# Reordering the first stage of a fused attention, expert and feed-forward kernel: tables and loads, products, scatters, and a PSUM bank for VectorE

## The chip, the cores and the metric

The kernel runs on one core of a Trainium2 chip. The metric is the time of one execution on the device in microseconds (us). In the rows PE is TensorE, PEld its weight loads, DVE VectorE, ACT ScalarE, POOL GpSimd, SP SyncE (which here issues most DMAs; SPq is its queue).

## The reference

Three computations follow one another, all in fp32. A recurrence over time with a state per head, then a mixture of 8 experts of which each token goes to one, then a gated feed-forward block.

```python
for t in range(S):                      # B=2, H=8, S=768, D=48
    cur = einsum('bhd,bhe->bhde', u * k[t], v[t])
    y[t] = einsum('bhd,bhde->bhe', r[t], state + cur)
    state = w * state + einsum('bhd,bhe->bhde', k[t], v[t])
x = y.transpose(0, 2, 1, 3).reshape(1536, 384)
logits = x @ w_gate; e = argmax(logits); gate = softmax(logits)[e]
x = gate * (relu(x @ w1[e]) @ w2[e])    # 8 experts, F=1024; up to `capacity` tokens each
g = x @ w_gate2
out = (g * sigmoid(g) * (x @ w_val)) @ w_out
```

## The kernel before

**Attention and routing (up to about 87 us).** The 1536 tokens are cut into NT = 12 tiles of 128, six (NCH) per batch. One loop, `for it in range(-4, NT + 1)` (L366 to L429), is a software pipeline: in iteration `it` it works on several tiles at once. For tile it+4 POOL makes the products `diag_pool` (L239 ruk = r*k, L240 ruk = ruk*u, L242 kd = k times powers of w), and SP loads r and k (`load_rk`, L131) into one of three buffers that these products have read before. For tile it+3 DVE scales the transposed r and k (`decay`, L234, RK) and sums ruk into the diagonal c (`diag_dve`, L246), and ACT writes 16 diagonal blocks (`diag_act`, L255). For tile it+2 TensorE forms A (`inner`, L262), of which DVE copies the lower triangle (L269), and the state's increment U (L277). The state Z is updated by DVE (L288) and POOL (L289). For tile `it` TensorE forms y (`outputs`, L297 and L303), ACT copies it to xT (`d_major`, L310), and TensorE turns it to token order with the logits beside it (`token_major`, L470, xl, in PSUM under the tag "xt" with two buffers). For tile it-1 `logits` sums the logits on DVE (L477, lg) and copies xu on ACT (L479).

Routing comes in groups of tiles, BATCHES = (0,3), (3,6), (6,8) and then one tile at a time. `route1` (L481 to L497) finds the expert by some small DVE operations (m, dif L491, eqr, oh L497) on lg, `place_pe` counts with TensorE (L510), `route2` (L514 to L543) gives each token its row in a table x_disp in DRAM. Each tile's x is then scaled by its gate on ACT (L550) and written to its rows by an indirect DMA that POOL issues (`scatter`, L551). `send()` does one such scatter at the start of an iteration, ahead of that iteration's work on POOL. The table has 1760 rows per expert, of which BLK = 224 are read at first.

The scatters are a chain: all write x_disp, and each waits for the one before to land. After scatter 7 the rows of expert 0 are loaded into xr0 (`x_load`, L625, on SP); scatter 8 waits for that load, and scatters 9, 10 and 11 follow. The load of expert 1's rows, xrs[1], here called xr1, waits for scatter 11. The rows of the last four tiles are added to expert 0's input by TensorE itself (`first_add`, L341), with xr0's rows (`first_rows`, L349).

**Experts (from about 87 us).** For each of 8 experts f runs over 8 steps up (`up_plain` L772 for expert 0, then L760) with a relu (L779 on ACT, L780 on DVE), and 8 steps down (L749, L750). The weights come in units, "raw" buffers of 128x768, RAWS = 10 of them, loaded on SP (`unit_load`, L606). `prefetch` (L642) loads units 0 to 7, one per iteration from it = 3 on; two more are loaded at the start of the experts. DVE and ACT split each unit into a high and a low part (L616, L617). At f = 0 of expert 0 `order()` (L805 and L898) does some small DVE work on the counts, at f = 1 `places()` (L815) and the load of xr1, at f = NF+3 = 11 `x_turn` transposes xr1 (L741).

**Feed-forward (to the end).** Products with w_gate, w_val and w_out, fed by what the experts left in DRAM.

The order of each engine's instructions is the order in which the code calls them; no scheduler changes it. The functions that the change touches:

Of the kernel before, what the change touches and what calls it, by code (L numbers as in the profile page):

```python
# [22 lines left out]
P = 128  # L23
# [24 lines left out]
RAWS, WS = 10, 6  # L48

# [15 lines left out]
class Kernel:  # L65
# [46 lines left out]
    def attention(self, st):  # L112
# [57 lines left out]
        Wm = tp.tile([P, HP, D], F32, name="Wm")  # L170
# [19 lines left out]
        nc.vector.tensor_copy(mask, tmpm)  # L190
        W2 = tp.tile([P, 2, HP, P], F32, name="W2")
# [13 lines left out]
        pbad = ps_1.tile([P, 1], F32, name="pbad", tag="xt", bufs=2)  # L205
# [14 lines left out]
        wps = ps_1.tile([P, HP, 2, 64], F32, name="wps", tag="xt", bufs=2)  # L220
# [6 lines left out]
        self.xl, self.xu, self.batches, self.to_scatter = {}, {}, BATCHES, []  # L227
# [8 lines left out]
        def diag_pool(i):  # L236
            r_t, k_t = rk[i % NB][:, 0], rk[i % NB][:, 1]
            ruk = ruks[i] = tp.tile([P, DM], F32, name="ruk", tag="ruk", bufs=2)
            nc.gpsimd.tensor_mul(ruk, r_t, k_t)  # L239
            nc.gpsimd.tensor_mul(ruk, ruk, u_b)  # L240
            if i % NCH < NCH - 1:
                nc.gpsimd.tensor_mul(kds[i % NB], k_t, wk_tok)  # L242

        def diag_dve(i):
            c = cc[i] = tp.tile([P, 2, HP], F32, name="c", tag="c", bufs=3)
            nc.vector.tensor_reduce(  # L246
                c.rearrange("p j h -> p h j"), ruks.pop(i).rearrange("p (h j d) -> p h j d", j=2, d=D), AX.X, ALU.add
            )
# [33 lines left out]
        def state_update(i):  # L282
            zn, hd = Z[(i + 1) % 2], slice(0, 64 + D)
            if i % NCH == 0:
                nc.vector.tensor_mul(zn[hd], U[hd], Wm[hd])
            else:
                zt = tp.tile([P, HP, D], F32, name="zt", tag="zt", bufs=2)
                nc.vector.tensor_add(zt[hd], U[hd], Z[i % 2][hd])  # L288
                nc.gpsimd.tensor_mul(zn[hd], zt[hd], Wm[hd])  # L289
# [24 lines left out]
        self.route_rooms()  # L314
        self.ones_bf = cp.tile([P, P], BF16, name="ones_bf")
# [11 lines left out]

        def late_tables():
            nc.vector.tensor_copy(Wm, sq[:, 7].unsqueeze(2).to_broadcast([P, HP, D]))
            self.route_tables(wg, tmpm, rev_i, cap_i)  # L330
            nc.vector.memset(self.ones_bf, 1.0)
# [26 lines left out]
        def send():  # L358

            if self.to_scatter:  # L360
                i = self.to_scatter[0][0]
                self.scatter()
                if i == NT - NLAST - 1:
                    self.x_load(0, self.xr0)

        for it in range(-4, NT + 1):  # L366

            send()
            batch = ends.get(it - 1)
            late = it - 1 >= NT - LATE  # L370
            if ok(it):
# [3 lines left out]
            if ok(it - 1):  # L375
                self.logits(it - 1)
# [17 lines left out]
            if it < 0 and ok(it + 3):  # L394
                decay(it + 3)
                load_T(it + 3 + NB)
            if ok(it + 3):
                diag_dve(it + 3)
                diag_act(it + 3)
            if ok(it + 4):  # L400
                diag_pool(it + 4)
                load_rk(it + 4 + NB)
            if ok(it + 2):
# [3 lines left out]
            if it >= 0 and ok(it + 3):  # L407
                decay(it + 3)
                load_T(it + 3 + NB)

            if it == NT - 5 or it == NT - 3:
                send()
# [13 lines left out]
            if it >= 3:  # L426
                self.prefetch(it - 3)
# [12 lines left out]

    def route_rooms(self):
# [3 lines left out]
        self.rev = tp.tile([P, E], F32, name="rev")  # L445
# [4 lines left out]
    def route_tables(self, wg, tmpm, rev_i, cap_i):  # L450
# [6 lines left out]
        nc.vector.tensor_copy(self.IW[:, :, 2 * D:], wg.rearrange("p (h e) -> p h e", e=E))  # L457
        nc.vector.tensor_copy(self.before, tmpm)
        nc.vector.tensor_copy(self.rev, rev_i)
        nc.vector.tensor_scalar(  # L460
            out=self.cap_f, in0=cap_i[:, 0:1], scalar1=float(E * ST), scalar2=None, op0=ALU.add
        )
        nc.vector.memset(self.ex[:, :, E:], 1e-9)
# [8 lines left out]
    def logits(self, i):  # L472
        nc, tp, xl = self.nc, self.tp, self.xl.pop(i)
        t = i - max(lo for lo, _ in self.batches if lo <= i)
        if t == 0:
            self.lg = tp.tile([P, NBT, E], F32, name="lg", tag="lg", bufs=2)
# [4 lines left out]
    def route1(self, lo, hi):  # L481
# [14 lines left out]
        nc.vector.tensor_reduce(m[:, 1], eqr, AX.X, ALU.max)  # L496
        nc.vector.tensor_tensor(oh, eqr, b3(m[:, 1]), ALU.is_equal)  # L497
# [16 lines left out]
    def route2(self, lo, hi):  # L514
# [3 lines left out]
        nc.vector.reciprocal(m[:, 2], m[:, 2])  # L518
# [7 lines left out]
            out=m[:, 3], in0=place, scalar=self.cap_f, in1=m[:, 2], op0=ALU.is_lt, op1=ALU.mult  # L526
        )

        def rows(out):
            nc.vector.scalar_tensor_tensor(  # L530
                out=out, in0=m[:, 1], scalar=-float(ST), in1=place, op0=ALU.mult, op1=ALU.add
# [13 lines left out]
    def scatter(self):  # L545
# [4 lines left out]
        self.nc.scalar.activation(xs, xu, AF.Copy, scale=scale)  # L550
        self.nc.gpsimd.indirect_dma_start(  # L551
            out=self.x_disp, out_offset=bass.IndirectOffsetOnAxis(ap=self.row[:, i:i + 1], axis=0), in_=xs,
            in_offset=None,
        )

# [86 lines left out]
    def prefetch(self, k):  # L642

        if k < 8:
            self.unit_load(0, k)
# [186 lines left out]
    def experts(self, st):  # L832
# [34 lines left out]
        n_loaded, n_split = 8, 1  # L867
# [171 lines left out]
    def general(self):  # L1039
# [3 lines left out]
        with ExitStack() as ss:  # L1043
# [13 lines left out]
            nc.gpsimd.iota(rev_i, pattern=[[-1, E]], base=E, channel_multiplier=0)  # L1057
            self.route_rooms()
# [122 lines left out]
```

## Time and profile before

| | us |
|---|---|
| median of 3 runs | 468.25 |
| lowest, highest | 466.6, 471.62 |
| the profiled execution | 467.29 |
| its span | 465.6 |
| mean granted clock of TensorE | 0.977 of full speed |

The rows of the trace come from the one profiled execution; its span is the time from its first to its last instruction, and the sums are made against its own 467.29 us. TensorE is busy for 437.9 us of the span (94%), VectorE for 295.4, ScalarE for 213.0, POOL for 173.8. [...]

### The profile page before, as it was taken

Reading aid. Unit: us, or ns where it says so; the run is one execution under the profiler, and the core shown is the slowest. Engines: PE = TensorE matmul, PEld = TensorE weight load, DVE = VectorE, ACT = ScalarE, POOL = GpSimd, SP = SyncE. Lnnn points to the kernel's source line nnn. Section 1 sums busy time; section 2 is a strip of 40 time slices with the busy share of each in tenths; the row PEclk is TensorE's granted clock in tenths of the full one; section 3 lists DMA queues with packets and bytes.
Section 4 is the critical chain, followed back from the end, with each engine's and each line's share of the span. In section 5 each row is a group of like instructions: output and inputs, shape, how many; then the busy total and the mean of one; then the engine's idle time right before and its main releaser. Section 6 shows DMA issues by size and latency. Waiting matters only on the chain. (4 is left out here: it accounts for less than half of the span.)

```text
span 465.6 us, 8417 instructions
## 1 busy us (share of the span) xinstructions
PE 437.9 (94%) x3211; PEld 422.6 (91%) x3211; DVE 295.4 (63%) x566; ACT 213.0 (46%) x469; POOL 173.8 (37%) x159
## 2 busy tenths in 40 slices
PE   7899959986999999999999999999999999999991
PEld 7688847876999999999998999999999999999991
DVE  6869778585798798889466698989857111111110
ACT  1667755452675666666455554334244032130310
POOL 6987563140111120000044445665454433233321
PEclk9799989998999999999999999999999999999998
DMA  7787931539998998750101333324300000100001
GB/s 261 254 285 249 337 132 59 186 117 288 360 328 206 283 295 203 265 195 1 69 1 68 137 86 119 126 78 136 124 14 1 34 18 1 52 0 35 19 18 39
DMA packets 24802, 63.78 MB, mean 137 GB/s; under 512 B 4784, under 2 KB 10032, under 8 KB 24752
## 3 DMA queue, kind: packets, MB, share of 16 engines
q1 hardware_dynamic: 22112, 57.43, 38.0%
q0 software_dynamic: 1920, 4.73, 2.8%
q10 hardware_dynamic: 720, 1.00, 0.9%
q8 instruction: 27, 0.44, 0.4%
q14 instruction: 23, 0.19, 0.1%
HBM read 55.67 MB, written 7.48 MB: 136 GB/s over the span
## 5 line engine op out<-in xcount | busy, mean ns | idle before, releaser
L984 POOL TENSOR_TENSOR al<-sg,ah 128x384 fp32r<-128x384 f32 x48 | 54.2, 1129 | 138.7 <-ACT ah L983 138.7
L617 DVE TENSOR_TENSOR wlo<-raw,whi 128x768 fp32r<-128x768 f32 x60 | 57.2, 954 | 12.2 <-ACT whi L616 10.1
L749 PE MATMUL py<-hc,whi 128*128 128x448 f32 x192 | 64.6, 377 | 0.0
L983 ACT CAST ah<-sg 128x384 fp32r<-128x384 f32 x48 | 24.7, 514 | 78.1 <-DVE sg L980 78.1
L760 PE MATMUL A<-xc,whi 128*128 128x224 f32 x336 | 56.6, 274 | 0.0
L750 PE MATMUL py<-hc,wlo 128*128 128x256 f32 x192 | 54.6, 284 | 0.0
L760 PEld LDWEIGHTS A<-xc,whi 128*128 128x128 f32 x336 | 51.1, 192 | 0.1
L616 ACT CAST whi<-raw 128x768 fp32r<-128x768 f32 x60 | 49.9, 838 | 2.8 <-DMA raw<-in_w 2.1
L997 PE MATMUL po<-w_out_hi,ah 128*128 128x384 f32 x144 | 48.6, 337 | 0.0
L999 PE MATMUL po<-w_out_hi,al 128*128 128x384 f32 x144 | 48.5, 337 | 0.0
L998 PE MATMUL po<-w_out_lo,ah 128*128 128x384 f32 x144 | 48.5, 337 | 0.0
L760 PE MATMUL A<-xc,wlo 128*128 128x224 f32 x168 | 46.2, 275 | 0.0
L749 PEld LDWEIGHTS py<-hc,whi 128*128 128x128 f32 x192 | 36.9, 192 | 2.7
L1006 DVE TENSOR_TENSOR acc<-acc,po 128x384 f32<-128x384 f32 x36 | 19.3, 546 | 30.9 <-PE po L999 30.9
L827 POOL DMA_INDIRECT ids<-tok,by_expert x12 | 14.6, 1213 | 62.7 <-DMA ids<-tok,by_expert 57.6
L980 DVE TENSOR_TENSOR sg<-A,sg 128x384 f32<-128x384 f32 x24 | 13.3, 554 | 37.9 <-PE A L977 30.2
L750 PEld LDWEIGHTS py<-hc,wlo 128*128 128x128 f32 x192 | 37.3, 194 | 0.0
L980 DVE TENSOR_TENSOR sg<-g,sg 128x384 f32<-128x384 f32 x24 | 13.3, 555 | 34.5 <-PE g L977 29.7
L255 ACT ACTIVATE AT<-ident,c 128x128 f32<-128x128 f32 x96 | 29.4, 390 | 11.7 <-DVE c L246 11.7
L779 ACT ACTIVATE hc<-A 128x224 fp32r<-128x224 f32 x64 | 23.1, 362 | 23.3 <-PE A L760 19.0
L760 PEld LDWEIGHTS A<-xc,wlo 128*128 128x128 f32 x168 | 32.3, 192 | 0.0
L979 ACT ACTIVATE sg<-A 128x384 f32<-128x384 f32 x24 | 11.7, 486 | 34.7 <-PE A L977 34.7
(171 smaller groups left out, 1132.1 us busy)
## 6 DMA issues: line engine op xcount, KB each, us to landing
raw<-in_w SPq DMA_DIRECT2D x62, 384.0 KB, 6.7
rkT<-in_rkT SPq DMA_DIRECT2D x12, 512.0 KB, 5.4
rk<-in_rk SPq DMA_DIRECT2D x12, 384.0 KB, 3.8
raw<-in_w_gate SPq DMA_DIRECT2D x6, 768.0 KB, 4.3
raw<-in_w_val SPq DMA_DIRECT2D x6, 768.0 KB, 4.5
raw<-in_w_out SPq DMA_DIRECT2D x6, 768.0 KB, 4.4
x_disp<-zero SPq DMA_DIRECT2D x8, 336.0 KB, 6.2
xr<-x_disp SPq DMA_DIRECT2D x8, 336.0 KB, 5.7
```

Source lines behind the costliest of these rows:

```text
L255: nc.scalar.activation(AT[i][:, j, hp], ident, AF.Copy, scale=c[:, j, hp:hp + 1])
L616: nc.scalar.copy(h_, raw)
L617: nc.vector.tensor_sub(l_, raw, h_.bitcast(F32))
L749: nc.tensor.matmul(ps[:, 0:2 * BLK], lhsT=wh, rhs=xc, start=first, stop=False, skip_group_check=True)
L750: nc.tensor.matmul(ps[:, 0:256], lhsT=wl, rhs=xc[:, 0:256], start=False, stop=last, skip_group_check=True)
L760: self.nc.tensor.matmul(ph[:, HI], lhsT=w[:, k, fs], rhs=x[1][:, k, half], start=(k == 0 and i == 0), stop=(k == KD - 1 and i == 2),)
L980: nc.vector.tensor_mul(sg, pg["w_val"], sg)
L983: nc.scalar.copy(h_, sg)
L984: nc.gpsimd.tensor_sub(l_, sg, h_.bitcast(F32))
L997: nc.tensor.matmul(po, lhsT=ah[:, ts_], rhs=wh, start=(i == 0), stop=False)
L998: nc.tensor.matmul(po, lhsT=ah[:, ts_], rhs=wl, start=False, stop=False)
L999: nc.tensor.matmul(po, lhsT=al[:, ts_], rhs=wh, start=False, stop=(i == len(parts) - 1))
```

## The change

The names in the changed kernel's rows are of its own lines. The parts:

- **Tables.** The tables for routing, which `late_tables` made in iteration -3 (L329 to L331, L453 to L463), are made before the powers of w; what needs w_gate and the capacity (`route_inputs`) comes in iteration -1. The tile Wm, w spread over the state, is gone: the multiplies read it by a broadcast from sq.
- **A bank in PSUM** (`psum_rooms`) holds lg, rev, the rank and the sum of routing, and u (`u_ps`). The buffers of the tag "xt" go from two to one.
- **Products.** ruk = ruk*u goes from POOL to DVE (in `diag_dve`); POOL's order is now ruk, the state's decay, kd.
- **Scatters.** `scale` (ACT) stays at the start of an iteration, `issue` (the DMA) comes at its end, behind the products, and only for the last iterations at once.
- **x ahead of the outputs.** `logits` (with xu's copy) comes before `outputs`; tile 2's diagonal comes behind xT in iteration 0; `inner` comes earlier in the iterations below 0.
- **Loads.** All ten raw units are loaded in iterations 3 to 8, ahead of xr0.
- **order() and places()** go from f = 0 and 1 to f = 3 and 5.

```diff
+PREFETCH = {3: [0], 4: [1], 5: [2], 6: [3], 7: [4, 5], 8: [6, 7, 8, 9]}
...
+        u_ps = self.psum_rooms(True)
+        self.route_rooms()
+        self.route_tables(tmpm, rev_i)
+        self.ones_bf = cp.tile([P, P], BF16, name="ones_bf")
+        nc.vector.memset(self.ones_bf, 1.0)
...
             nc.gpsimd.tensor_mul(ruk, r_t, k_t)
-            nc.gpsimd.tensor_mul(ruk, ruk, u_b)
+
+        def keys_pool(i):
             if i % NCH < NCH - 1:
-                nc.gpsimd.tensor_mul(kds[i % NB], k_t, wk_tok)
+                nc.gpsimd.tensor_mul(kds[i % NB], rk[i % NB][:, 1], wk_tok)
...
+            nc.vector.tensor_mul(ruk, ruk, u_ps)
             nc.vector.tensor_reduce(
...
-                nc.gpsimd.tensor_mul(zn[hd], zt[hd], Wm[hd])
...
+        nc.vector.tensor_copy(u_ps, u_b)
...
+        def state_decay(i):
+            zn, hd = Z[(i + 1) % 2], slice(0, 64 + D)
+            nc.gpsimd.tensor_mul(zn[hd], self.zt[hd], sq[hd, 7].unsqueeze(2).to_broadcast([64 + D, HP, D]))
...
         for it in range(-4, NT + 1):
-
-            send()
+
+            if self.to_scatter:
+                self.scale()
+                if it >= NT - 3:
+                    issue()
...
+            if ok(it - 1):
+                self.logits(it - 1)
             if ok(it):
                 outputs(it)
                 if not late:
                     d_major(it)
-            if ok(it - 1):
-                self.logits(it - 1)
+            if it == 0:
+                diag_act(2)
...
             if ok(it + 4):
                 diag_pool(it + 4)
+            if has_state(it + 1) and (it + 1) % NCH:
+                state_decay(it + 1)
+            if ok(it + 4):
+                keys_pool(it + 4)
                 load_rk(it + 4 + NB)
...
+            if self.scaled:
+                issue()
...
-            if it == -3:
-                late_tables()
+            if it == -1:
+                self.route_inputs(wg, cap_i)
...
-            if it >= 3:
-                self.prefetch(it - 3)
+            self.prefetch(it)
...
+        bank = self.ps_1.tile([P, 512], F32, name="bank")
+        n = NBT * E
+        self.lgs = [bank[:, i * n:(i + 1) * n].rearrange("p (t e) -> p t e", e=E) for i in range(2)]
...
-        xl = self.xl[i] = self.ps_1.tile([P, HP, 2 * D + E], F32, name="xl", tag="xt", bufs=2)
+        xl = self.xl[i] = self.ps_1.tile([P, HP, 2 * D + E], F32, name="xl", tag="xt")
...
-        n_loaded, n_split = 8, 1
+        n_loaded, n_split = RAWS, 1
...
-        load(2, 0)
...
-                if e == 0 and f == 0:
-                    order()
-                if f == 1:
+                if e == 0 and f == 1:
+                    xrs[1] = self.x_block(ST)
+                if f == (5 if e == 0 else 1):
                     if e == 0:
-                        xrs[1] = self.x_block(ST)
                         self.places()
...
+                if e == 0 and f == 3:
+                    order()
```

How the order of instructions moves is shown at three places. First POOL in iteration 6 before, from scatter 2 to scatter 3 (rk_88 holds r and k of tile 10):

```order
L551 DMA x_disp<-xu,row 14080x384
L289 TENSOR_TENSOR Z_135<-zt,Wm 112x192
L239 TENSOR_TENSOR ruk<-rk_88 128x384
L240 TENSOR_TENSOR ruk<-ruk,u_b 128x384
L242 TENSOR_TENSOR kd_126<-rk_88,wk_tok 128x384
L551 DMA x_disp<-xu,row 14080x384
```

and POOL in the changed kernel, from scatter 1 to scatter 2, with the same tile's products:

```order
L589 DMA x_disp<-xu,row 14080x384
L246 TENSOR_TENSOR ruk<-rk_88 128x384
L371 TENSOR_TENSOR Z_134<-zt,sq 112x192
L250 TENSOR_TENSOR kd_126<-rk_88,wk_tok 128x384
L589 DMA x_disp<-xu,row 14080x384
```

The product by u_b is gone, ruk stands ahead of Z, and tile 10's products follow scatter 1 instead of scatter 2. Second, SP from the last loads of r and k (rk), of their transposes (rkT) and of v on, before; the first xr is xr0, the second xr1:

```order
L131 DMA rk_89<-in_rk 128x768
L127 DMA rkT_85<-in_rkT 128x1024
L134 DMA v_all<-in_v 128x3x384
L606 DMA raw<-in_w 128x768
L127 DMA rkT_86<-in_rkT 128x1024
L606 DMA raw<-in_w 128x768 x4
L625 DMA xr<-x_disp 112x2x384
L606 DMA raw<-in_w 128x768 x4
L625 DMA xr<-x_disp 112x2x384
```

and in the changed kernel:

```order
L133 DMA rk_89<-in_rk 128x768
L129 DMA rkT_85<-in_rkT 128x1024
L136 DMA v_all<-in_v 128x3x384
L648 DMA raw<-in_w 128x768
L129 DMA rkT_86<-in_rkT 128x1024
L648 DMA raw<-in_w 128x768 x8
L667 DMA xr<-x_disp 112x2x384 x2
```

The four raw loads that stood between xr0 and xr1 now stand ahead of xr0. Third, DVE in the prologue, from RK of tile 0 (rkT_84) to RK of tile 1 (rkT_85), before:

```order
L234 TENSOR_TENSOR RK<-rkT_84,W_146 128x2x256 x2
L246 TENSOR_REDUCE c<-ruk 128x4x2
L329 COPY Wm<-sq 128x192
L453 COPY IW<-ident 128x4x48 x2
L457 COPY IW<-wg 128x4x8
L458 CAST before<-tmpm 128x128
L459 CAST rev<-rev_i 128x8
L460 TENSOR_SCALAR cap_f<-cap_i 128x1
L463 MEMSET ex 128x3
L331 MEMSET ones_bf 128x128
L234 TENSOR_TENSOR RK<-rkT_85,W_146 128x1024
```

and in the changed kernel:

```order
L335 COPY bank<-u_b 128x384
L241 TENSOR_TENSOR RK<-rkT_84,W_157 128x2x256 x2
L255 TENSOR_TENSOR ruk<-ruk,bank 128x384
L256 TENSOR_REDUCE c<-ruk 128x4x2
L241 TENSOR_TENSOR RK<-rkT_85,W_157 128x1024
```

The tables no longer stand between c and RK of tile 1; the copy of u into the bank and the multiply by it are new.

## Rows read from the trace of the kernel before

**Rows 1.** Windows: us, busy us of PE, PEld, DVE, ACT, POOL, PEclk, DMA, GB/s.

```profile
50.00:60.00 10.00, 9.29 (x148) 7.86 (x146) 6.73 (x21) 5.70 (x16) 6.06 (x8) 1.00 0.98 375
60.00:70.00 10.00, 5.43 (x71) 4.74 (x69) 9.09 (x15) 6.36 (x20) 6.25 (x7) 0.76 0.23 86
114.00:450.00 336.00, 335.04 (x2145) 332.02 (x2144) 209.03 (x319) 152.63 (x307) 108.30 (x83) 1.00 0.36 116
```

**Rows 2.** Timeline around tiles 8 and 9: start, us, engine, line, work [idle before <-releaser].

```profile
52.56 1.12 PE L470 MATMUL xl<-IW,xT 128*128 128x104 f32 x8
...
57.05 1.01 POOL L551 DMA_INDIRECT x_disp<-xu,row  x1 [3.72 <-ACT xu L550]
...
60.74 0.55 DVE L246 TENSOR_REDUCE c<-ruk 128x8 f32<-128x384 f32 x1 [1.67 <-POOL ruk L240]
...
63.56 0.18 DVE L477 TENSOR_REDUCE lg<-xl 128x8 f32<-128x32 f32 x1
...
63.78 0.17 DVE L490 TENSOR_REDUCE m<-lg 128x2 f32<-128x16 f32 x1
...
63.79 1.16 PE L262 MATMUL A<-RK 48*128 48x128 f32 x16 [2.08 <-DVE lg L477]
...
63.98 2.31 DVE L491 TENSOR_TENSOR dif<-lg,m 128x16 f32<-128x16 f32 x1
...
67.44 0.17 PE L510 MATMUL pos<-oh,before 128*128 128x16 bf16 x1 [2.49 <-DVE oh L497]
...
67.53 2.02 PE L470 MATMUL xl<-IW,xT 128*128 128x104 f32 x8
```

**Rows 3.** Timeline of the scatters, the loads of xr and their users.

```profile
42.97 1.16 POOL L551 DMA_INDIRECT x_disp<-xu,row  x1 [0.18 <-issue]
...
63.67 1.01 POOL L551 DMA_INDIRECT x_disp<-xu,row  x1 [2.00 <-DVE RK L234]
...
67.98 1.01 POOL L551 DMA_INDIRECT x_disp<-xu,row  x1 [0.62 <-issue]
...
78.19 1.01 POOL L551 DMA_INDIRECT x_disp<-xu,row  x1 [1.83 <-ACT ex L492]
...
82.28 0.33 SPq L625 DMA_DIRECT2D xr<-x_disp  x1
...
82.65 1.88 SPq L606 DMA_DIRECT2D raw<-in_w  x4
...
86.31 0.96 POOL L551 DMA_INDIRECT x_disp<-xs,row  x1 [7.11 <-DVE m L518]
...
86.73 1.57 PE L349 MATMUL A<-ident,xr 112*128 112x112 f32 x12
...
92.48 0.96 POOL L551 DMA_INDIRECT x_disp<-xs,row  x1 [5.21 <-DVE offs L810]
...
104.10 0.33 SPq L625 DMA_DIRECT2D xr<-x_disp  x1
...
108.83 0.79 PE L741 MATMUL px<-ident,xr 112*128 112x112 f32 x6 [4.30 <-DMA xr<-x_disp]
```

**Rows 4.** Timeline of the first iterations: tables, RK(1), outputs(0), one xu copy.

```profile
11.28 0.59 DVE L329 COPY Wm<-sq 128x192 f32<-128x192 f32 x1
...
13.45 1.86 DVE L234 TENSOR_TENSOR RK<-rkT,W 128x1024 f32<-128x1024 f32 x1
...
18.46 1.95 PE L297 MATMUL y<-RK,zero 48*48 48x128 f32 x16
...
28.41 0.49 ACT L479 COPY xu<-xl 128x384 f32<-128x384 f32 x1
```

**Rows 5.** Durations: source view of L240, and a group of the page's part 5.

```profile
L240 POOL TENSOR_TENSOR ruk<-ruk,u_b x12: 995/1018/2051, 9.0 to 66.3; 128x384 f32<-128x384 f32 x12
...
L1006 DVE TENSOR_TENSOR acc<-acc,po 128x384 f32<-128x384 f32 x36 | 19.3, 546 | 30.9 <-PE po L999 30.9
```

**Rows 6.** Waits of TensorE from 0 to 114 us: total, times, longest.

```profile
PE A L772 <- DVE hc L780: 1.4, 2, 1.0
```

More of the change, by code (lines that the diff above doesn't have):

```diff
@@ L204, in attention @@
         )
-        pbad = ps_1.tile([P, 1], F32, name="pbad", tag="xt", bufs=2)
+        pbad = ps_1.tile([P, 1], F32, name="pbad", tag="xt")
         nc.tensor.matmul(pbad, lhsT=ones, rhs=nbad, start=True, stop=True)
@@ L219, in attention @@
         wk_tok = tp.tile([P, DM], F32, name="wk_tok")
-        wps = ps_1.tile([P, HP, 2, 64], F32, name="wps", tag="xt", bufs=2)
+        wps = ps_1.tile([P, HP, 2, 64], F32, name="wps", tag="xt")
         for hp in range(HP):
@@ L356, in attention, with issue @@
         ends = {hi - 1: (lo, hi) for lo, hi in BATCHES}
-        def send():
-            if self.to_scatter:
[L361 to L366, printed above, removed]
-            send()
+        def issue():
+            i = self.scaled[0][0]
+            self.issue()
+            if i == NT - NLAST - 1:
+                self.x_load(0, self.xr0)
+        def state_decay(i):
+            zn, hd = Z[(i + 1) % 2], slice(0, 64 + D)
+            nc.gpsimd.tensor_mul(zn[hd], self.zt[hd], sq[hd, 7].unsqueeze(2).to_broadcast([64 + D, HP, D]))
+        for it in range(-4, NT + 1):
+            if self.to_scatter:
+                self.scale()
+                if it >= NT - 3:
+                    issue()
             batch = ends.get(it - 1)
             late = it - 1 >= NT - LATE
+            if ok(it - 1):
+                self.logits(it - 1)
             if ok(it):
@@ L439, in attention, with psum_rooms @@
         self.unit_split(4)
+    def psum_rooms(self, u=False):
+        bank = self.ps_1.tile([P, 512], F32, name="bank")
+        n = NBT * E
+        self.lgs = [bank[:, i * n:(i + 1) * n].rearrange("p (t e) -> p t e", e=E) for i in range(2)]
+        self.rev = bank[:, 2 * n:2 * n + E]
+        self.rank = bank[:, 2 * n + E:2 * n + E + NBT]
+        self.sum = bank[:, 2 * n + E + NBT:2 * n + E + 2 * NBT]
+        return bank[:, 512 - DM:] if u else None
     def route_rooms(self):
@@ L474, in logits @@
         t = i - max(lo for lo, _ in self.batches if lo <= i)
-        if t == 0:
-            self.lg = tp.tile([P, NBT, E], F32, name="lg", tag="lg", bufs=2)
+        self.lg = self.lgs[sum(lo <= i for lo, _ in self.batches) % 2]
         nc.vector.tensor_reduce(self.lg[:, t], xl[:, :, 2 * D:].rearrange("p h e -> p e h"), AX.X, ALU.add)
@@ L525, in route2 @@
         nc.vector.scalar_tensor_tensor(
-            out=m[:, 3], in0=place, scalar=self.cap_f, in1=m[:, 2], op0=ALU.is_lt, op1=ALU.mult
+            out=m[:, 3], in0=place, scalar=self.cap_f, in1=self.sum[:, 0:n], op0=ALU.is_lt, op1=ALU.mult
         )
@@ L530, in rows @@
             nc.vector.scalar_tensor_tensor(
-                out=out, in0=m[:, 1], scalar=-float(ST), in1=place, op0=ALU.mult, op1=ALU.add
+                out=out, in0=self.rank[:, 0:n], scalar=-float(ST), in1=place, op0=ALU.mult, op1=ALU.add
             )
@@ L543, in route2, with scale @@
         self.to_scatter += [(i, m[:, 3, i - lo:i - lo + 1]) for i in range(lo, hi)]
-    def scatter(self):
+    def scale(self):
         i, scale = self.to_scatter.pop(0)
@@ L554, in scatter @@
         )
+    def scatter(self):
+        self.scale()
+        self.issue()
     def count(self):
@@ L640, in x_part_plain, with prefetch @@
         (self.nc.vector.tensor_copy if k == 1 else self.nc.scalar.copy)(xc[:, k], px[k][:, HI])
-    def prefetch(self, k):
-        if k < 8:
-            self.unit_load(0, k)
+    def prefetch(self, it):
+        for n in PREFETCH.get(it, []):
+            self.unit_load(n // 8, n % 8)
     def convert_all(self):
```

49 lines of the change are left out of this document (27 added, 22 removed).

## The prediction

> **What bounds the kernel now.** All sums are made against the profiled execution: 467.29 us, of which the span is 465.6. The median of the three runs shown, 468.25, lies 1.0 above it.
>
> I began with the busy times by stretch. From 114 to 450 us TensorE is busy for 335.04 of 336.00 us [rows 1], and the change touches no work of that part; so the program ends as much earlier as TensorE comes past 114 us earlier, and only what happens before it counts. There TensorE is not full: from 60 to 70 us it is busy for 5.43 of 10, at a mean granted clock of 0.76 [rows 1].
>
> Next, what TensorE waits for before 114. Around tiles 8 and 9 the timeline shows 2.08 us in front of the products A (L262, at 63.79) and 2.49 in front of the positions (L510, at 67.44) [rows 2]. The last wait of the part is 4.30 us in front of L741, at 108.83, for the load of xr1 [rows 3]. That last one decides how the rest is to be read: TensorE was there at 104.53, and whatever it gains before is lost again at L741 unless xr1 comes earlier too.
>
> So the third view is the timeline of what brings xr1. It is a chain of DMAs. By the waits written into the program each scatter waits until the one before has landed, the load of xr0 waits for scatter 7, scatter 8 for that load, the load of xr1 for scatter 11. Its issues stand in [rows 3]: scatter 0 at 42.97, 3 at 63.67, 4 at 67.98, 7 at 78.19, xr0 at 82.28, scatter 8 at 86.31, 9 at 92.48, xr1 at 104.10, used at 108.83; 65.86 us in all. The steps differ. The three from scatter 0 to 3 take 20.70 us, 6.90 each; the three from 4 to 7 take 10.21, 3.40 each. The first three lie where the DMA engines move 375 GB/s at a share of 0.98, the others where they move 86 GB/s at 0.23 [rows 1]. I call them loaded and idle steps.
>
> **The change part by part.** *Tables.* Between the reduction of c and RK(1), DVE works from 11.28 to 13.45 [rows 4] on nine table operations, 2.17 us. They move to a place ahead, where DVE waits for w_dm, or to a later iteration; one multiply by the bank comes in. No row shows DVE multiplying 128x384 by a PSUM operand; the nearest is acc<-acc,po, 0.546 us [rows 5]. So outputs(0), at 18.46 [rows 4], come 2.17 - 0.55 = 1.6 us earlier. Bounds: 0, if the loads of rkT set that place; 3.5, if RK(1)'s 1.86 [rows 4] leaves the path as well.
>
> *The product on POOL.* L240 took 1.02 us on POOL, twelve times [rows 5]; it becomes 0.55 on DVE. At tile 8 it is on the path: scatter 2 leaves POOL idle for 3.72 us until 57.05, L240 follows it, DVE waits 1.67 for it until 60.74, and TensorE's 2.08 at 63.79 is what comes of that (DVE makes RK, which A needs, behind c; the row names the operation after RK) [rows 2]. In the new order the products stand ahead of the scatter, and L240 is gone, so I let the 2.08 go. Of the twelve times 0.55 I charge nothing, since DVE is busy 6.73 of 10 us from 50 to 60 [rows 1]; without that cover they are 6.6 us of DVE.
>
> *The bank in PSUM.* dif (L491) takes 2.31 us at 63.98, the operation before it 0.17 [rows 2]. Both are tiny; dif has two operands in SBUF, and I read the row so that it was held up while POOL worked. With lg in the bank it has one, so I take it at 0.18, and the 2.49 at 67.44 goes. Behind that wait the clock is at the lower level: L470 takes 2.02 us at 67.53 and 1.12 at 52.56 [rows 2]. [...]
>
> The sum is unaffected by what follows in this paragraph. The rows show no price for reading PSUM: the reduction from PSUM (L477) takes 0.18, the one from SBUF (L490) 0.17 [rows 2]. [...]
>
> *xu ahead of xT, and one buffer for xl.* xu takes 0.49 us on ACT [rows 4]; ahead of xT it delays it by at most that, and by nothing where ACT is idle. It frees xl sooner, which the single buffer needs, since the next L470 has to wait for xl's readers. At tile 8 L477 reads it at 63.56, and the next L470 comes at 67.53 [rows 2]. I take 0; bounds 0 and +1.0 a tile.
>
> *order() and places() later.* They stand in front of a relu that TensorE waits for, 1.4 us at L772 [rows 6]; at f 3 and 5 their work lies beside products already fed. -1.4 for TensorE.
>
> TensorE alone thus comes to L349, now at 86.73 [rows 3], 1.6 + 2.08 + 2.49 + 2 = 8.2 us earlier, at 78.5.
>
> *The chain* has four terms.
> T1, its start. Scatter 0 follows POOL's products of tile 7 after 0.18 us [rows 3]. Now tile 8's two products stand ahead of it, but two L240 are gone, so it moves with the prologue: -1.6, bounds 0 and -3.5.
> T2, the three loaded steps, 20.70. A load of r and k into a used buffer waits for POOL's product of the tile before, so without L240 the loads start earlier: 1.02 for each of about four tiles, 4 us, and the burst with them. But the four raws issued at 82.65 behind xr0 [rows 3] now belong to the burst: 4 x 128 x 768 x 4 bytes = 1.57 MB, 4.2 us at 375 GB/s. So its end stays where it is, while the chain's start has moved little. Ends: -10.5, if all three steps become idle ones (20.70 - 10.2); +4.2, if the scatters pay the added bytes in full. I take -2.0, half of the way that the earlier start gives, since the nearest rows, the loaded steps, show that the scatters do wait for the burst.
> T3, scatter 3 to 4, 4.31, with L240 in front of the scatter on POOL: 3.40, -0.9.
> T4, scatter 8 to 9, 92.48 - 86.31 = 6.17 [rows 3], behind those four raws: 3.40 without them, -2.8.
> The load of xr0 (82.28 to 86.31, 4.03) and the rest stay.
> Sum: -1.6 - 2.0 - 0.9 - 2.8 = -7.3; xr1 is used at 101.5.
>
> Both sides together: xr0 is issued at 82.28 - 4.5 = 77.8 and there at 81.8; TensorE, at L349 from 78.5, waits 3.3 us, a wait that is new. From there to L741 it needs 104.53 - 86.73 - 1.4 = 16.4, comes at 98.2 and waits 3.3 again. The chain decides twice: 467.29 - 7.3 = 460.0, and what TensorE gains beyond it turns into these two waits.
>
> On T2's upper end: the loaded steps are twice the idle ones, which shows that scatters share the engines with the burst but not how. [...]
>
> **Rivals.** *A, the chain gets out of the way.* The burst, started earlier, is over before the scatters: T2 is -10.5, xr1 is ready 15.8 earlier, and TensorE is the bound. It comes to L741 at 104.53 - 8.2 - 1.4 = 94.9 instead of 108.83: -13.9, 453.4. For it: idle steps of 3.40 [rows 3]. Against: 1.57 MB more in front of xr0.
>
> *B, slower.* The single buffer ties each L470 to xu on ACT and lg on DVE, and DVE has 0.55 more per tile. If L470 waits 1.0 us in each of twelve tiles, TensorE and the chain (whose tiles come from it) go 12 later: -7.3 + 12 = +4.7, 472.0. It decides from 7.3 / 12 = 0.6 a tile. For it: DVE busy for 9.09 of 10 us from 60 to 70 [rows 1], 2.3 of it dif. Against: the 3.97 us between L477 and L470 at tile 8 [rows 2].
>
> *C, nothing to measure.* The scatters pay for the four raws: T2 is +4.2, the sum -1.1, 466.2, and TensorE waits at L349 and L741 for all that it gained. For it: SP's order puts raws 6 to 9 ahead of xr0. Against: they are issued in iteration 8, when scatters 0 to 3 are mostly out.
>
> **How the numbers follow.** A measurement of this kernel can tell about 1%, 4.7 us, from no change. The forecast, 460.0 with its own range of 456 to 463, has 0.60, A 0.18, C 0.17, B 0.05. So faster by over 1%: 0.60 + 0.18 = 0.78; within 1%: 0.17; slower: 0.05. For the range A takes the low end to 450 (453.4, some 2 less with 3.5 in place of 1.6 for the prologue, rounded down), C the high end to 466; B is left out.
>
> **What would show it.** Right: outputs(0) near 16.9; dif under 0.3 us and no wait at L262 and L510 around tile 8; scatter 8 to 9 near 3.4; TensorE waiting about 3 us at L349 for xr0 and 3 at L741 for xr1. Wrong: no wait at L741 (A); scatters 0 to 3 taking over 20.7 us and a wait at L741 above 4 (C); a wait of L470 in most tiles (B); or a step at 16.9 that does not come.

## The result and the profile after

The changed kernel takes 463.0 us (median of 4 runs, 462.68 to 463.33) against 468.25 (466.6 to 471.62): a ratio of 0.9893, interval 0.9852 to 0.9934. That is 5.3 us or 1.1% less, with an interval to both sides of the 1% that the forecast set for "faster", and the time is 3 us above its 460.0: at the top of its own range of 456 to 463, and about half way to the 466.2 of rival C. The profiled execution took 462.68 us with a span of 461.0, 4.6 less than before; the sums below are made between the two profiled executions.

First the busy times by stretch of the changed kernel (columns as in [rows 1]):

```profile
103.03:109.00 5.97, 5.97 (x23) 5.62 (x24) 2.83 (x6) 2.50 (x5) 1.24 (x1) 0.50 1.04 396
109.00:445.00 336.00, 335.04 (x2145) 332.01 (x2145) 209.58 (x318) 151.97 (x306) 106.44 (x82) 1.00 0.37 114
```

The long rest of the program is the same 335.04 us of TensorE in 336.00 as in [rows 1], only 5 us earlier, so the bound was read rightly: only what happens ahead of this stretch counts. In front of it, behind the wait at L783 (L741 before), stands a stretch at a mean granted clock of 0.50. The kernel before has one at the same place, but only part of it at 0.50, with a mean of 0.67:

```profile
108.83:114.00 5.17, 5.17 (x25) 4.87 (x26) 2.04 (x4) 1.78 (x5) 0.96 (x1) 0.67 0.87 315
```

Next the timeline of the chain, the answer to [rows 3] (L589 is the scatter, L667 the load of xr, L353 first_rows, L783 the transposition of xr1):

```profile
41.91 1.16 POOL L589 DMA_INDIRECT x_disp<-xu,row  x1 [2.93 <-ACT xu L583]
...
62.65 1.01 POOL L589 DMA_INDIRECT x_disp<-xu,row  x1 [4.67 <-ACT ex L525]
...
66.24 0.96 POOL L589 DMA_INDIRECT x_disp<-xu,row  x1 [2.58 <-DVE ohs L575]
...
76.30 1.01 POOL L589 DMA_INDIRECT x_disp<-xu,row  x1 [1.83 <-DMA x_disp<-xu,row]
...
78.92 0.33 SPq L667 DMA_DIRECT2D xr<-x_disp  x1
...
82.62 0.96 POOL L589 DMA_INDIRECT x_disp<-xs,row  x1 [5.31 <-DVE bank L551]
...
83.18 1.57 PE L353 MATMUL A<-ident,xr 112*128 112x112 f32 x12
...
85.97 0.96 POOL L589 DMA_INDIRECT x_disp<-xs,row  x1 [2.39 <-ACT x_plain L682]
...
89.35 1.25 POOL L589 DMA_INDIRECT x_disp<-xs,row  x1 [2.42 <-ACT hc L821]
...
94.94 1.18 POOL L589 DMA_INDIRECT x_disp<-xs,row  x1 [4.33 <-ACT hc L821]
...
97.74 0.33 SPq L667 DMA_DIRECT2D xr<-x_disp  x1
...
103.03 1.38 PE L783 MATMUL px<-ident,xr 112*128 112x112 f32 x6 [3.97 <-DMA xr<-x_disp]
```

Piece by piece against [rows 3], with the forecast beside it:

| piece of the chain | before | after | forecast | measured |
|---|---|---|---|---|
| start of scatter 0 (T1) | 42.97 | 41.91 | -1.6 | -1.06 |
| scatters 0 to 3 (T2) | 20.70 | 20.74 | -2.0 | +0.04 |
| scatter 3 to 4 (T3) | 4.31 | 3.59 | -0.9 | -0.72 |
| scatters 4 to 7 | 10.21 | 10.06 | 0 | -0.15 |
| scatter 7 to the issue of xr0 | 4.09 | 2.62 | 0 | -1.47 |
| xr0 to scatter 8 | 4.03 | 3.70 | 0 | -0.33 |
| scatter 8 to 9 (T4) | 6.17 | 3.35 | -2.8 | -2.82 |
| scatter 9 to the issue of xr1 | 11.62 | 11.77 | 0 | +0.15 |
| xr1 to its use | 4.73 | 5.29 | 0 | +0.56 |
| sum | | | -7.3 | -5.80 |

xr1 is used 5.80 us earlier. From there to the end of the span it was 465.6 - 108.83 = 356.77 us and is 461.0 - 103.03 = 357.97: 1.20 more, and -5.80 + 1.20 = -4.60 is the difference of the spans. The 1.20 is the clock: the six matmuls of L741 took 0.79 us behind a wait of 4.30 [rows 3], those of L783 take 1.38 behind 3.97. From there to the first product of expert 1 it is 114.88 - 108.83 = 6.05 us before, at a mean granted clock of 0.72, and 110.24 - 103.03 = 7.21 after, at 0.59, so 1.16 of the 1.20 lies in this stretch; multiplied by its clock it is 4.4 us before and 4.3 after.

Last, what TensorE waits for from 0 to 114 us in the changed kernel (total, times, longest; only the three largest):

```profile
PE px L783 <- DMA xr<-x_disp: 4.0, 1, 4.0
PE xl L504 <- ACT xT L320: 2.3, 2, 1.2
PE A L272 <- DVE RK L241: 1.5, 2, 0.9
```

The waits of 2.08 and 2.49 around tiles 8 and 9 [rows 2] are gone. The wait for xr1 stands there as before, and there is none for xr0 at L353. In place of the old ones there are waits for xT and for RK.

### The profile page after: what moved, and what is told of

The parts are those of the page before. It is cut to its first block, busy times and chain, and to the rows that moved or that the text cites. A ratio compares the mean times of both kernels' runs of the same rounds, so it can differ in the third digit from the quotient of the medians.

```text
span 461.0 us, 8436 instructions
## 1 busy us (share of the span) xinstructions
PE 436.4 (95%) x3211; PEld 421.9 (92%) x3211; DVE 297.7 (65%) x578; ACT 213.0 (46%) x469; POOL 157.4 (34%) x147
## 3 DMA queue, kind: packets, MB, share of 16 engines
q0 software_dynamic: 1920, 4.73, 2.8%
```

## Experiments

Two theories were tried first. The chain of scatters to xr1 sets the end, and the four raws beside it were the part of it that could go; or TensorE's own side (tables, products, bank) made the gain. Ratios are to the kernel before, timed beside each run.

**e1_raws_only**: the kernel before with the order of the raw loads alone.

```diff
+PREFETCH = {3: [0], 4: [1], 5: [2], 6: [3], 7: [4, 5], 8: [6, 7, 8, 9]}
...
-            if it >= 3:
-                self.prefetch(it - 3)
+            self.prefetch(it)
...
-        n_loaded, n_split = 8, 1
+        n_loaded, n_split = RAWS, 1
...
-        load(2, 0)
```

> The kernel before with one part of the change alone: all ten raw loads ahead of xr0. Theory (the chain of scatters to xr1 sets the end, and the four raws beside it were its largest removable part): the chain from scatter 7 on shortens by about 4 us, xr1 is used about 4 us earlier, TensorE's wait at L741 falls from 4.30 to under 1.5 us, and the time is about 464.5 us (3 to 4.3 us less than before), although nothing on TensorE's side was touched. Rival (the gain came from the tables, the products and the bank): the wait at L741 stays at 4 us and the time within 1.5 us of before.

467.35 us, ratio 0.9984 (0.9953 to 1.0016); the profiled execution took 464.64. Its timeline (L742 is the transposition of xr1, L626 the load of xr, L494 the operation behind dif):

```profile
64.07 2.19 DVE L494 SCALAR_TENSOR_TENSOR eqr<-dif,rev 128x16 f32<-128x16 f32 x1
64.68 0.59 POOL L291 TENSOR_TENSOR Z<-zt,Wm 112x192 f32<-112x192 f32 x1
65.23 0.99 POOL L241 TENSOR_TENSOR ruk<-rk 128x384 f32<-128x384 f32 x1
...
100.59 0.33 SPq L626 DMA_DIRECT2D xr<-x_disp  x1
...
106.15 0.74 PE L742 MATMUL px<-ident,xr 112*128 112x112 f32 x6
```

and two of its waits of TensorE:

```profile
PE U L279 <- POOL kd L244: 2.1, 1, 2.1
...
PE U L279 <- DMA v_all<-in_v: 1.2, 1, 1.2
```

The chain gained as expected: xr1 is issued at 100.59 instead of 104.10 [rows 3], and the wait at the transposition is gone altogether. But TensorE itself only comes there at 106.15; before it came at 104.53. It waits for kd and for v_all, which the trace of before does not have among its large waits, and keeps the old waits of tiles 8 and 9. (The two new waits belong to the execution rather than to the edit: e10, which is the kernel before up to the transposition, has them too, 2.2 and 0.6 us.) So the profiled execution, the fastest of its ten, gains 2.7 and no more, and the median nothing that can be measured. The theory was right on the chain and wrong on the time: TensorE, the other bound, came 4.30 us ahead of xr1's 108.83 in the trace of before and starts only 2.68 ahead of it here.

**e2_raws_back**: the changed kernel with the four raws behind xr0.

```diff
-PREFETCH = {3: [0], 4: [1], 5: [2], 6: [3], 7: [4, 5], 8: [6, 7, 8, 9]}
+PREFETCH = {3: [0], 4: [1], 5: [2], 6: [3], 7: [4], 8: [5], 9: [6], 10: [7], 11: [8, 9]}
```

> The changed kernel with the four raws 6 to 9 put back behind xr0 on SP, as before. Theory (chain): scatter 8 to 9 takes about 6 us again instead of 3.35, xr1 is used about 4 us later, TensorE waits about 8 us at L783, the time is about 467 us (+4). Rival (TensorE's own side made the gain): within 1 us of 463.0. [...]

469.25 us, ratio 1.002 (0.9986 to 1.0055). Its timeline:

```profile
80.18 1.88 SPq L648 DMA_DIRECT2D raw<-in_w  x4
...
83.73 0.96 POOL L589 DMA_INDIRECT x_disp<-xs,row  x1 [6.33 <-DVE m L550]
...
90.06 0.96 POOL L589 DMA_INDIRECT x_disp<-xs,row  x1 [5.36 <-ACT hc L821]
...
108.48 1.38 PE L783 MATMUL px<-ident,xr 112*128 112x112 f32 x6 [7.92 <-DMA xr<-x_disp]
```

As the theory said: scatter 8 to 9 takes 6.33 again, TensorE waits 7.92 us, and the whole gain of the change is gone although every edit on TensorE's side is in. TensorE comes to L783 at 108.48 - 7.92 = 100.56, 4 us before it did in the kernel before, for nothing.

The two runs and the two kernels make a square. The transposition of xr1 starts when the later of two is there, TensorE or xr1. The times and the span are those of one profiled execution each, the ratio that of all runs:

| kernel | TensorE there | transposition starts | who was late | span | ratio |
|---|---|---|---|---|---|
| before | 104.53 | 108.83 | xr1 | 465.6 | 1 |
| raws alone (e1) | 106.15 | 106.15 | TensorE | 462.9 | 0.9984 |
| all but the raws (e2) | 100.56 | 108.48 | xr1 | 466.4 | 1.002 |
| the change | 99.06 | 103.03 | xr1 | 461.0 | 0.9893 |

The ratios show that neither part alone brings anything and both together do. Who was late is read from single executions, and e1's is a fast one.

The price of the burst: scatters 0 to 3 take 60.94 - 41.37 = 19.57 us in e2 with four raws fewer, 20.74 in the changed kernel. The other runs with all eight raws and the changed order of POOL have 19.37 (e3), 19.54 (e7), 20.96 (r_after), 21.23 (e4), 21.58 (e6), 21.83 (e5), 21.99 (e9) and 22.05 (e8). So 1.57 MB more cost less than one execution differs from the next (2.7 us), below the 4.2 us of full payment.

**e3_bank_sbuf**: the changed kernel with the values of routing in SBUF.

```diff
-        n = NBT * E
+        u_ps, n = bank[:, 512 - DM:], NBT * E
+        bank = self.tp.tile([P, 512 - DM], F32, name="room")
...
-        return bank[:, 512 - DM:] if u else None
+        return u_ps if u else None
```

> The changed kernel with the routing values (logits, rev, rank, sum) in SBUF again; u stays in PSUM. Theory (chain): the time stays within 1 us of 463.0, whatever the routing operations take, since TensorE waits 3.97 us at L783 anyway. For the reading of dif: an operation of two SBUF operands beside a busy POOL takes over 0.5 us, the same beside an idle POOL 0.17 to 0.18; in the changed kernel POOL is idle at dif of tiles 6 and 7, so most stay at 0.18. Rival (the bank made the gain): 2 to 4.5 us slower, with a wait of over 2 us in front of the positions.

464.97 us, ratio 0.9916 (0.9886 to 0.9945): 2.0 us above the change, where the theory allowed 1, but the intervals overlap and it is not told apart from the change; its profiled execution took 461.72. Groups of its instructions by line (mean ns of one before the last bar):

```profile
L525 DVE TENSOR_TENSOR dif<-room,m 128x8 f32<-128x8 f32 (+2 forms) x7 | 1.2, 172 | 0.2
...
L524 DVE TENSOR_REDUCE m<-room 128x1 f32<-128x8 f32 (+2 forms) x7 | 1.2, 168 | 0.2
```

and those of the changed kernel, where the same two read the bank:

```profile
L523 DVE TENSOR_REDUCE m<-bank 128x1 f32<-128x8 f32 (+2 forms) x7 | 1.2, 172 | 0.4 <-DVE bank L510 0.2
L524 DVE TENSOR_TENSOR dif<-bank,m 128x8 f32<-128x8 f32 (+2 forms) x7 | 1.2, 172 | 0.2
```

No gain by the bank is shown: with dif back on two SBUF operands it takes 172 ns too, and the trace has no product on POOL beside it any more. As to the reading of [rows 2]: in e1 the long operation is eqr (2.19 us, two SBUF operands) and not dif, and it starts 0.61 us ahead of POOL's Z (64.68), where dif started 0.73 ahead of it before (63.98 and 64.71). So the length goes with the place beside POOL's work and not with one instruction; in e3, beside the issue of a scatter alone (1.29 us from 61.09), dif and eqr of the same tiles take 0.17, at 61.82 and 62.03.

**e4_turn_late**: the changed kernel, xr1 transposed one step later.

```diff
-                turn = NF + 2 if e else NF + 3
+                turn = NF + 2 if e else NF + 4
```

> The changed kernel with the transposition of xr1 one step of f later for expert 0 (f = 12 instead of 11). Theory: TensorE fills about 1.9 us of the wait of 3.97 with products, the wait at L783 falls to about 2 us, and the stretch at the lower clock behind it is as long or shorter: 460 to 461.5 us. Rival (the wait only moves: the casts of xr1 come too late for expert 1's first products): 463 us, with a new wait of about 2 us at the first product of expert 1.

462.65 us, ratio 0.9885 (0.984 to 0.9931). The wait fell to 3.3 instead of about 2; a step is 4.17 / 4 = 1.04 us and not 1.9, and xr1 was 1.0 later in this execution (used at 104.06). Between the theory and the rival, nearer to no change.

**e5_xu_behind**: the changed kernel with logits() behind outputs() and d_major() again.

```diff
-            if ok(it - 1):
-                self.logits(it - 1)
             if ok(it):
                 outputs(it)
                 if not late:
                     d_major(it)
+            if ok(it - 1):
+                self.logits(it - 1)
```

> The changed kernel with the copy of xu (and the logits) behind the outputs and xT again, on ACT and DVE. Theory: xu ahead of xT is what makes TensorE wait 1.19 and 1.12 us for xT in iterations 4 and 7; both waits fall below 0.6 us, outputs(5) to (8) start 0.5 to 1.5 us earlier, and the end stays within 1 us of 463.0 because scatters, not TensorE, decide. Rival (TensorE's order still counts): 461.5 us or less. Second rival (the single buffer of xl needs xu early): new waits of L504 for xu, 464 us or more.

463.4 us, ratio 0.9899 (0.9861 to 0.9937). One wait of TensorE:

```profile
PE xl L504 <- ACT xu L512: 2.5, 2, 1.3
```

The wait of L504 is as long as in the changed kernel (2.3), with another name on it: there xT is late because xu stands ahead of it on ACT, here xu is late and holds the one buffer of xl. Which stands first is worth nothing that the runs can tell; both stand on ACT behind the same scaling.

**e6_no_act_raws**: the changed kernel without ACT's two raw loads in expert 0's first steps.

```diff
-                load(2, e * NU + (f + 1) // 2, nc.scalar if e == 0 and f < 4 else None)
+                if e or f > 3:
+                    load(2, e * NU + (f + 1) // 2)
```

> The changed kernel without the two raw loads that ACT issues at f = 1 to 3 (units 10 and 11 go to SP behind xr1). Theory (chain): they are what makes the step from scatter 10 to 11 5.59 us instead of 3.38; without them it is about 3.4, xr1 is issued about 2.2 us earlier, TensorE's wait at L783 falls from 3.97 to about 1.8, the time is about 461 us. Rival (the late units are missed): same wait, or a new one of TensorE in expert 1, 463 us or more.

464.99 us, ratio 0.9922 (0.9881 to 0.9963). Scatters 10 and 11:

```profile
92.39 1.70 POOL L589 DMA_INDIRECT x_disp<-xs,row  x1 [2.42 <-ACT whi L658]
...
97.84 1.38 POOL L589 DMA_INDIRECT x_disp<-xs,row  x1 [3.75 <-DVE hc L822]
```

The step is 5.45 us without any raw beside it: the theory is not borne out. 0.74 of it is the issue (1.70 instead of 0.96, beside a DVE operation of two SBUF operands that starts at 92.30). For the rest, some 1.3 us over the usual 3.4, the DMA view of 92.39 to 97.80 has this (queue, kind: packets, MB, share; then the scatter's us from issue to landing):

```profile
q8 instruction: 1, 0.02, 1.2%
...
x_disp<-xs,row POOLq DMA_INDIRECT x1, 4.7
```

A packet of 16 KB of the kind instruction lies from 94.72 to 95.78, inside the scatter's own 64 packets, which take from 94.67 to 96.58: 1.91 us. Scatters with nothing beside their packets mostly need 0.67 to 0.70 for them and land after 2.6. Windows with short steps hold such a packet too, but not, or for no more than 0.03 us, beside the scatter's own packets: in the changed kernel one lies from 73.03 to 73.99, ahead of the packets of scatter 6, which take from 74.50 to 75.19. So the long step of this run has another neighbour than that of the changed kernel, and what ACT's two raws cost there (its 64 packets take 1.62 us beside them and an instruction packet) stays open. From the transposition to the end this kernel needs 463.8 - 104.35 = 359.45, 1.5 more than the change, with a new wait of 1.0 for a relu in expert 1, which fits units that come late.

**e7_z_ahead**: the changed kernel with scatter 6 at the end of iteration 9, behind the state's decay.

```diff
-                if it >= NT - 3:
+                if it >= NT - 2:
                     issue()
```

> The changed kernel with the state's decay for tile 11 ahead of scatter 6 on POOL (the scatter goes to the end of iteration 9). Theory: the wait of 1.15 us of outputs(11) for Z and the lower clock behind it (outputs(11) at 1.68 and 1.95 us instead of 1.08) go, first_rows (L353) start 1 to 2.5 us earlier unless xr0 holds them, and the end stays within 1 us of 463.0, the gain turning up as a longer wait at L783 (5 to 6 us). Rival (TensorE's side decides at that place): 461 us or less.

464.23 us, ratio 0.992 (0.9886 to 0.9955). Here is what it undoes, in the changed kernel:

```profile
72.97 0.96 POOL L589 DMA_INDIRECT x_disp<-xu,row  x1 [2.39 <-DVE m L563]
...
73.96 0.51 POOL L371 TENSOR_TENSOR Z<-zt,sq 112x192 f32<-112x192 f32 x1
...
74.52 1.68 PE L307 MATMUL y<-RK,Z 48*48 48x128 f32 x16 [1.15 <-POOL Z L371]
```

and the same places in e7:

```profile
61.91 1.95 PE L307 MATMUL y<-RK,Z 48*48 48x128 f32 x16
...
77.18 1.08 PE L307 MATMUL y<-RK,Z 48*48 48x128 f32 x16
84.26 1.57 PE L353 MATMUL A<-ident,xr 112*128 112x112 f32 x12
```

The wait for Z is gone and outputs(11) run at full clock (1.08 us at 77.18, and a mean granted clock of 1.00 from 70 to 80), as expected; but in this execution the clock was low at tile 8 (1.95 us at 61.91, and a mean of 0.72 from 60 to 70), so L353 comes at 84.26 and not earlier than 83.18. The end does not move, which both the theory and the accident explain; the wait at L783 is 4.23 and not the 5 to 6 that the theory asked for.

**e8_joined**: the edits of e5, e6 and e7 together.

> The three edits of the runs e5, e6 and e7 together. Theory: the chain gains 2.2 us from the loads by ACT and TensorE is ready for it, so about 460.5 us, with a wait at L783 of 2 to 4 us left. Rival (the edits only exchange waits): 462.5 to 463.5 us.

464.39 us, ratio 0.9939 (0.9903 to 0.9974): the rival, if anything worse, as e6 already made likely.

**e9_turn_last** and **e10_before_turn**: the transposition of xr1 three steps later, in the changed kernel and in the kernel before, and **r_after**, the changed kernel again, on the same chip.

```diff
-                turn = NF + 2 if e else NF + 3
+                turn = NF + 2 if e else NF + 6
...
                     self.x_part(x, f - turn - 1)
+                if e == 0 and f == 2 * NF - 1:
+                    self.x_part(x, 1)
+                    self.x_part(x, 2)
```

> The changed kernel with the transposition of xr1 three steps of f later for expert 0 (f = 14 instead of 11), and the casts of all three parts at f = 15. In the changed kernel four steps took 4.17 us (94.89 to 99.06), so three are 3.1 us of products ahead of the wait. Theory (xr1, by the chain, sets the end): the wait at L783 falls from 3.97 to about 0.9 us, the clock behind it no longer falls or for a shorter time, and the time is 3 to 5 us less than the changed kernel's on the same chip. Rival (the wait only moves): a new wait of 2 us or more at expert 1's first products for the casts, and the time within 1.5 us of the changed kernel's.

> The kernel before with the same late transposition of xr1 and nothing of the change. Theory (the chain and TensorE's own work are two bounds close to each other, the chain 4.30 us behind): the wait at L741 falls from 4.30 to about 1.2 us, the time by 3 to 4 us, which is most of what the whole change brings. Rival (what TensorE does before 100 us decides): within 1.5 us of before.

> The changed kernel as it is, beside the two runs above on one chip, for the comparison: about 463 us, ratio 0.989 to before; the wait at L783 near 4 us.

e9: 462.5 us, ratio 0.9864 (0.9815 to 0.9913); r_after: 463.93 (461.0 to 468.14), ratio 0.9886 (0.9798 to 0.9973); e10: 468.81, ratio 0.9995 (0.9957 to 1.0034). Waits of TensorE in e9:

```profile
PE A L802 <- DVE hc L822: 1.3, 2, 1.1
PE px L783 <- DMA xr<-x_disp: 1.3, 1, 1.3
```

and in e10:

```profile
PE A L760 <- DVE hc L780: 2.6, 1, 2.6
...
PE A L760 <- DVE xc L633: 0.5, 1, 0.5
```

In e9 the wait fell to 1.3 as expected and a wait of 1.3 for a relu of expert 1 came up; the ratio is lower than r_after's, but the intervals overlap: a better kernel is not shown. In e10 the wait of 4.30 is gone altogether and the time stays: 3.1 us come back as waits for expert 1's relu and casts, which this edit itself pushes together. (Its profiled execution, 471.63, is the slowest of its ten, and xr1 is issued at 107.64 in it; the waits show where time goes, not how much in the median.) By the median the rival holds there.

**e11_product_on_pool**: the changed kernel with ruk*u on POOL.

```diff
             nc.gpsimd.tensor_mul(ruk, r_t, k_t)
+            nc.gpsimd.tensor_mul(ruk, ruk, u_b)
...
-            nc.vector.tensor_mul(ruk, ruk, u_ps)
...
-        nc.vector.tensor_copy(u_ps, u_b)
```

> The changed kernel with one part taken back: the product ruk*u is on POOL again (and u is not copied to the bank); POOL's order, the scatters behind the products, the loads and the tables stay as changed. Theory (the chain sets the end, TensorE has 4 us in hand at L783): c waits for POOL at some tiles, TensorE comes to L783 1 to 3 us later and waits 1 to 3 us instead of 4, and the time stays within 1.5 us of the changed kernel's (463 us). Rival (the product's move carries the gain): 466 us or more, with waits of 2 us at A (L272) as before.

465.62 us, ratio 0.9963 (0.9936 to 0.9991): about two thirds of the gain gone by the two ratios, where the theory allowed 1.5 us and the rival asked for all of it. Its timeline:

```profile
43.90 1.16 POOL L588 DMA_INDIRECT x_disp<-xu,row  x1 [0.17 <-ACT xu L511]
...
105.05 1.38 PE L782 MATMUL px<-ident,xr 112*128 112x112 f32 x6 [4.30 <-DMA xr<-x_disp]
```

TensorE still waits 4.30 us for xr1. TensorE is there at 100.75, 1.69 later than in the changed kernel, and still ahead of xr1; so the product counts through the chain, not through TensorE: scatter 0 starts 2.0 us later than in the changed kernel, and xr1 is used 2.0 later.

## Why the prediction was right or wrong

**The bound: right, and half of the story.** The chain to xr1 decided, and TensorE waits 3.97 us for it (forecast about 3). e2 shows it: with the chain long again nothing is left of the change. What the forecast did not have is how near the other bound was: it gave the four terms to the chain and counted TensorE's gain as spare, while e1 shows that without TensorE's part the chain's gain stops at 106.15. Only both together give 5 us.

**The sum: within the range partly by luck.** The four terms together measured -4.56 of the -7.3. What no term had is -1.24 on the chain and +1.20 for the clock behind it, and these two cancel. Over all the traces only T1 and T4 stand clear of the spread between executions; T2 and T3 do not.

**T4: right.** -2.8 forecast, -2.82 measured, and e2 puts it back (6.33). In every trace with raws behind xr0 the step is 6.17 to 6.33, in every other 3.34 to 3.37. Four raw loads beside one scatter are the largest single piece.

**T1: right in size for the wrong reason.** outputs(0) start at 16.73, 1.73 earlier (forecast 1.6), so the tables did what was worked out. But e11 keeps that gain (outputs(0) at 16.60) and has scatter 0 at 43.90, later than before. What moved scatter 0 by 1.06 is the product gone from POOL, which sets the pace between; the tables' gain is spent on the way. The other nine traces with the changed order have scatter 0 at 41.20 to 41.82 and once, in e9, at 43.22; the two other traces with the order of before have it at 43.48 (e1) and 44.20 (e10).

**T2: the step that failed.** -2.0 was forecast from loads that start 4 us earlier; +0.04 was measured. The loads did not start earlier: SP issues the burst

```profile
50.53 0.33 SPq L129 DMA_DIRECT2D rkT<-in_rkT  x1
...
50.90 5.36 SPq L648 DMA_DIRECT2D raw<-in_w  x8
```

at 50.90, against 50.78 before, because the load of rkT in front of it waits for DVE's RK of the tile before, not for POOL's product: RK takes 1.93 us from 48.57, to 50.50, and the load starts at 50.53. And DVE's pace had gained next to nothing there. Behind this stands, in the changed kernel:

```profile
37.65 2.42 DVE L241 TENSOR_TENSOR RK<-rkT,W 128x1024 f32<-128x1024 f32 x1
37.98 1.00 POOL L250 TENSOR_TENSOR kd<-rk,wk_tok 128x384 f32<-128x384 f32 x1
...
40.12 1.16 PE L272 MATMUL A<-RK 48*128 48x128 f32 x16 [0.87 <-DVE RK L241]
...
40.95 0.61 ACT L583 ACTIVATE xu<-xu,m 128x384 f32<-128x384 f32 x1 [1.98 <-DVE m L558]
...
42.47 1.14 PE L504 MATMUL xl<-IW,xT 128*128 128x104 f32 x8 [1.19 <-ACT xT L320]
```

RK takes 2.42 us beside POOL's products, twice its usual 1.21 (as at 59.05, with POOL idle). TensorE waits for it, and so does ACT: its scaling needs DVE's m, which comes behind RK. xu and xT follow the scaling, and TensorE waits another 1.19 for xT. The nine other traces with this order of DVE and POOL (all but e11's) have the same RK at 2.40 to 2.42 us. outputs(3) were 2.2 us earlier than before (32.91 against 35.14), outputs(5) only 0.6 (44.04 against 44.65). The wait for xT, which the forecast priced at 0 within 0 to 1.0 a tile, came twice, 1.19 and 1.12. The -2.0 itself is smaller than the spread: scatters 0 to 3 take 19.37 to 22.05 in the nine traces with this order and these loads, and 20.70 and 21.40 (e10) with those of before. So the traces show no gain, and could not have told one of 2.0 from the spread in one pair. Rival C's mechanism in full (4.2 us paid for the added bytes) is not seen in e2 and the other runs; its signs, over 20.7 us and a wait above 4, were all but met (20.74 and 3.97) and could not tell it from a T2 of nothing. A's is not seen either: the loaded steps are as long as they were.

**T3: right in this pair of executions, not shown.** -0.72 for -0.9, but the step that took 3.59 here takes 3.70 to 5.06 in the nine other traces of this order, and 4.31, 5.05 (e1) and 5.19 (e10) in that of before.

**What no term had.** From scatter 7 to the issue of xr0 it went from 4.09 to 2.62, which no step priced. The DMA view of this stretch has a packet of the kind instruction beside the scatter before, and none after (first the kernel before, from 78.19 to 82.28, then the changed one, from 76.30 to 78.92; last the us from issue to landing):

```profile
q8 instruction: 1, 0.02, 2.3%
...
x_disp<-xu,row POOLq DMA_INDIRECT x1, 4.1
```

```profile
x_disp<-xu,row POOLq DMA_INDIRECT x1, 2.6
```

In the kernel before that packet lies from 79.49 to 80.97, and the 64 packets of scatter 7 take from 79.78 to 81.80, 2.02 us; after, they take 0.68. It is not the place of the raws: e3 and e7 have them ahead of xr0 and take 3.39 and 3.21. In all five traces in which an instruction packet lies beside the packets of scatter 7 (before, e10, e2, e3, e7) the step is 3.21 to 4.09, in the nine others 2.59 to 2.63. So this gain came by where an instruction packet fell. Against it, 0.56 more for xr1's own load and 1.20 for the clock behind L783.

**The new wait at L349: wrong.** 3.3 us for xr0 were forecast, none came. TensorE was forecast there at 78.5 and was at 83.18, after xr0: of its 8.2 us it kept 3.55. No run shows the 2 us that the 8.2 has for a higher clock at L470. What the traces show in its place: before, a granted clock of 0.50 from 65.23 to 72.05, with TensorE busy for 4.61 us; in the changed kernel 1.00 from 64 to 74.85 and 0.50 from there to 78.25, with TensorE busy for 3.40. At half the clock the difference of 1.21 is worth an estimated 0.6 us. TensorE had 6.2 of the 8.2 at tile 9 (outputs(9) at 64.08 against 70.28), and lost 1.15 of these to the wait for Z behind scatter 6 and 1.5 behind it at the clock of 0.50, where the two halves of outputs(11) take 1.68 and 1.95 instead of 1.08 each. The forecast priced scatters ahead of Z at nothing for the last tiles, where the change still issues them at the top.

**The bank: dif as forecast, the credit wrong.** dif takes 0.17 us, as forecast, but so it does in e3 from SBUF. For the same reduction the rows show 172 ns from the bank and 168 from SBUF: 4 ns. And the 2.49 at L510 goes without the bank too: in e3 the longest wait there is 1.1.

**Rival B (slower): no.** L504 waits twice, 2.3 us in all, and not in each of twelve tiles; the rows name xT there, not the buffer.

## What to carry to other kernels

Where the last wait of a stage is for a chain of DMAs and the engine's own work ends a few microseconds before it, both are the bound: write down when each would be there, edit by edit, and credit an edit only with the move of the later one. Two edits that each measure as nothing can be worth 1% together. Loads that nobody waits for yet belong in front of a chain of dependent small DMAs or behind it, not beside it: in this kernel four of them cost one step 2.8 us, while the same bytes in an already loaded stretch cost nothing that could be told from the spread. And before a step of one trace is put down to an edit, look for the same step in every other trace: here that took T2, T3 and the gain at scatter 7 off the list.

## What the runs showed of the hardware that was not expected

An instruction of two SBUF operands on DVE beside POOL's work can take over 2 us instead of 0.17 (dif 2.31 in [rows 2], eqr 2.19 in e1), or twice its time (RK, 2.42 for 1.21). It is not tied to a line: in e1 dif starts 0.12 us earlier, at 63.86, and takes 0.17, and eqr behind it is the long one.

A single packet of 16 KB of the kind instruction, beside the packets of an indirect scatter, goes with 0.6 to 1.5 us more for the step: scatter 7 above, 3.21 to 4.09 us in five traces of fourteen and 2.59 to 2.63 in the others.

Halves of outputs that take 1.95 us instead of 1.08, which the changed kernel has at a granted clock of 0.50, come at different tiles in executions of nearly the same program: at outputs(11) in the changed kernel (1.68 and 1.95 us, behind waits of 1.37 and 1.15; clock 0.50 from 74.85 to 78.25), at outputs(8) in e7 (1.95 twice; mean clock 0.72 from 60 to 70), at outputs(5) in e5 (1.95 twice from 43.89), each time behind a wait of TensorE of over 1 us (1.19 and 1.25 in e7 and e5). r_after waits 1.74 for Z in front of outputs(11) and runs their first half in 1.08 and the second in 1.78 (mean clock 0.83 from 70 to 80). Not every such wait is followed by it: the changed kernel waits 1.19 at 42.47, and its granted clock is 1.00 from 40 to 50. In the two halves of outputs it costs 1.5 us in the changed kernel and 1.7 in e7 and e5, about what several of these edits were meant to bring; single profiled executions of one kernel (461.0 and 460.2 us of span for the changed kernel) differ by 0.8.
